# One load of output weights, a grouped early projection and useless matmuls at the end of a decode kernel

## The chip, the cores and the metric

The kernel runs on one core of a Trainium2 chip. The metric is the device time of one execution in microseconds (us). Beside it every run lists the *span* of the core, from its first to its last instruction. The device time is about 2.0 us longer than the span, and that difference scatters by some tenths from run to run, so where a few tenths matter this text compares spans.

PE is the engine that multiplies matrices, DVE and ACT are the two that copy and do elementwise work, SP issues the loads. "Granted clock" is the share of full speed that PE's clock was given; in the records it is only ever 1.0 or 0.5. I call PE *warm* at 1.0 and *cold* at 0.5.

## The reference

A decode step of attention with a key and value cache, then a small MLP, both behind adaptive layer norms.

```python
# B=8, D=512, 32 query heads, 8 key/value heads, 8192 positions, head size 128, F=1792
h = layernorm(x) * (1 + ca) + sa
q = (h @ wq)                               # 32 heads of 128
p = softmax(q @ k_cache^T * Dh**-0.5)      # k_cache, v_cache: 8 x 8 x 8192 x 128 bf16
x = x + ga * ((p @ v_cache) @ wo)          # wo: 4096 x 512 = 4 MB
h = layernorm(x) * (1 + cb) + sb
x = x + gb * (relu(h @ w1 + b1)**2 @ w2 + b2)
```

The two caches are 268 MB, and everything else is 15 MB.

## The kernel before

Each batch has four key units and four value units of 4 MB each, loaded through a ring of four slots. I count units from 0, so the last batch ends with value units 2 and 3. Value unit 3 of the last batch comes in four smaller loads (chunks of 64, 32, 16 and 16 tiles), and the MLP weights (`ring<-in_B_w`) are loaded behind it. The output projection for the first three units is done early, while the last unit is still arriving.

```python
# the output weights: 24 heads in 4 KB runs, 8 heads in 1 KB runs
d_woe = dma("sync", s_woe, lambda e: e.dma_start(
    wo_e, A_wo[0:24 * DH, :].rearrange("(g p j) n -> p g (j n)", g=6, p=128)))
d_wo = dma("sync", s_wo, lambda e: e.dma_start(
    wo_sb[:, 24:32, :], A_wo[24 * DH:, :].rearrange("(h dh) n -> dh h n", dh=DH)))
# ...
def pe_stream(n, at):            # n useless 512-column matmuls, to keep PE busy
    # ...
def project(k_oP):               # early projection: 96 matmuls of 32 columns
    for g in range(6):
        for j in range(4):
            for k in range(KT):
                op("tensor", lambda e, g=g, j=j, k=k: e.matmul(
                    attn_w[:, k, :, :], wo_sb[:, 4 * g + j, k * 128:(k + 1) * 128], wide(oP[:, j, g, :]),
                    start=(g == 0 and j == 0 and k == 0), stop=False, skip_group_check=True),
                    [k_oP, d_woe])
# ... a value unit (all but the very last): 32 matmuls of 512 columns in four column groups
for m in range(32):
    cg = m % 4
    t = op("tensor", lambda e, p=p, m=m, cg=cg, vt=vt, Obank=Obank: e.matmul(
        Obank[32 * cg:32 * (cg + 1), :], lhs[:, p, 32 * m:32 * m + 32],
        vt[:, 4 * m:4 * m + 4, :], start=(m < 4), stop=(m >= 28), tile_position=(0, 32 * cg)), ...)
# ... behind it a copy to SBUF, four selection matmuls, and (last batch, unit 2) the early projection
    if lastb and p == NP - 2:
        project(early([norm_last, k_all] + stg_free + hold))
# ... the last value unit: 24 wide matmuls (chunks 0 and 1), 16 narrow (chunk 2), 16 narrow (chunk 3)
    direct(96, 112, 2, True, False)
    # ...
    t = direct(112, 128, 3, False, True)
    for x in range(8):           # final projection: the last 8 heads
        for k in range(KT):
            k_attn = op("tensor", ...)
# ... layer norm, W1 (56 matmuls), squared ReLU, W2 (56 matmuls, wait for the last loads), output
```

## Time and profile before

| | before |
|---|---|
| device time, first three runs | 670.03 us (669.75 to 670.32) |
| span of the profiled run | 668.1 us |
| bytes moved, mean rate | 283.86 MB, 425 GB/s |
| PE busy | 74% of the span |

From the page of the kernel before: the busy share of the DMA engines in 40 slices of the span (a digit is tenths, 9 is 90% or more), and the packet counts.

```profile
DMA  9999999999999999999999999999999999999996
...
DMA packets 12961, 283.86 MB, mean 425 GB/s; under 512 B 1266, under 2 KB 2323, under 8 KB 4372
```

The DMA engines are busy from the first slice to the last but one. So a microsecond saved inside the loop on PE is worth nothing, and one saved in the stream of bytes is worth a microsecond, provided that the work behind the last byte keeps up.

The output-weight loads of the kernel before, from the view of DMA issues (size, median us from issue to landing):

```profile
wo_sb<-in_A_wo_dram SPq DMA_DIRECT2D x1, 3072.0 KB, 45.5
wo_sb<-in_A_wo_dram SPq DMA_DIRECT2D x1, 1024.0 KB, 48.0
```

The end of the span decides. PE's timeline there, kernel before (start us, duration us, engine, line, operation, output<-inputs, shapes, count, and in brackets the idle time before the group and what ended it):

```profile
644.90 1.91 PE L607 MATMUL PS<-ring,Pm 128*32 128x512 bf16 x32 [1.49 <-DMA ring<-in_A_v_cache_dram]
...
649.09 2.69 PE L517 MATMUL PS<-KTb,wo_sb 128*128 128x32 bf16 x96 [0.51 <-DVE KTb L511]
...
651.90 1.74 PE L659 MATMUL PS<-ring,Pm 128*32 128x512 bf16 x16
...
656.47 0.99 PE L682 MATMUL PS<-oTn,wo_sb 128*128 128x8 bf16 x32 [0.29 <-DVE oTn L677]
...
664.07 1.01 PE L730 MATMUL PS<-KTb,ring 128*128 128x8 bf16 x24 [0.67 <-DMA ring<-in_B_w_dram]
```

Value unit 2 (L607) starts when its load lands at 644.86; the early projection (L517) follows, then the last value unit (L659), the final projection (L682), and W2 (L730), which waits 0.67 us for its weights. The chain that ended last in the kernel before says the same (start us, length us, what):

```profile
648.00 16.02 DMA ring<-in_B_w_dram
664.02 0.05 issue
664.07 0.59 PE PS L730 x16
```

So the loads end the span, and PE is close behind them. The granted clock around this place, kernel before, from the table of windows with the windows cut where the clock may change (window and length in us; busy us and instruction counts of PE, PEld, DVE, ACT, POOL; granted clock; DMA share; GB/s):

```profile
646.52:649.93 3.41, 1.71 (x61) 1.22 (x54) 1.25 (x3) 0.00 (x0) 0.00 (x0) 1.00 0.96 402
649.93:653.34 3.41, 3.41 (x90) 2.37 (x85) 0.00 (x0) 0.00 (x0) 0.00 (x0) 0.50 1.01 403
653.34:656.75 3.41, 2.83 (x77) 1.95 (x70) 0.88 (x2) 0.00 (x0) 0.00 (x0) 1.00 1.02 405
```

A window in which PE was half busy (1.71 of 3.41 us) is followed by one at clock 0.50, and a fully busy one by 1.00.

### The profile page before, as it was taken

The numbers are of one execution on the slowest core, as the hardware profiler recorded it, in microseconds if no ns is written. First come the engines' busy times: TensorE is split into PE (matmuls) and PEld (weight loads), VectorE is DVE, ScalarE is ACT, GpSimd is POOL, SyncE is SP. The second block draws the span as 40 slices with busy tenths as digits, with TensorE's granted clock in tenths as the row PEclk, the third lists the DMA queues.
The fourth block names the chain that finished last, engine by engine and source line by source line (L and its number), as shares of the span: only waits on it lengthen the run. The fifth ranks groups of instructions, "written<-read, shape, count | busy, mean of one in ns | idle before, by whom it ended". The sixth has DMA issues, their size and how long they took to land.

```text
span 668.1 us, 15500 instructions
## 1 busy us (share of the span) xinstructions
PE 494.0 (74%) x7076; PEld 339.1 (51%) x7076; DVE 301.6 (45%) x569; ACT 258.7 (39%) x289; POOL 17.7 (3%) x71
## 2 busy tenths in 40 slices
PE   3494964898639983699638985499746996389866
PEld 2383731685228741577317752287414773177534
DVE  1262741466216651367315672167513673156622
ACT  2151640466205660166404661066502664046610
POOL 7300000000000000000000000000000000000000
PEclk9696996799869997599968998699977999579996
DMA  9999999999999999999999999999999999999996
GB/s 376 435 403 438 420 429 438 428 430 430 439 428 432 428 439 428 432 430 438 428 434 428 438 428 434 428 438 428 434 428 438 430 432 428 438 434 430 426 420 263
DMA packets 12961, 283.86 MB, mean 425 GB/s; under 512 B 1266, under 2 KB 2323, under 8 KB 4372
## 3 DMA queue, kind: packets, MB, share of 16 engines
q1 hardware_dynamic: 12900, 283.65, 99.1%
q8 instruction: 10, 0.16, 0.1%
q10 hardware_dynamic: 48, 0.02, 0.0%
q14 instruction: 3, 0.02, 0.0%
HBM read 283.66 MB, written 0.01 MB: 425 GB/s over the span
## 4 chain that ended last, share of the span: by engine, by line
PE 51%; DMA 37%; ACT 7%; DVE 4%; SPq 1%; issue 1%
PE PS L467 36%; DMA ring<-in_A_k_cache_dram 34%; PE PS L484 9%; ACT P_sb L553 5%; DMA ring<-in_B_w_dram 2%; PE PS L607 2%; ACT KTb L472 1%; SPq L642 1%; DVE m L491 1%; DVE O_sb L613 1%; PE PS L565 1%; PE PS L457 1%; DVE Pm L579 0%; PE PS L585 0%; DVE rhs_r L582 0%
## 5 line engine op out<-in xcount | busy, mean ns | idle before, releaser
L472 ACT ACTIVATE KTb<-PS 128x1024 bf16<-128x1024 bf16 x192 | 196.5, 1024 | 332.9 <-PE PS L467 332.9
L467 PE MATMUL PS<-IDENT,ring 128*128 128x128 bf16 x4096 | 268.1, 228 | 50.5 <-DMA ring<-in_A_k_cache_dram 50.5
L467 PEld LDWEIGHTS PS<-IDENT,ring 128*128 128x128 bf16 x4096 | 247.4, 102 | 99.2 <-DMA ring<-in_A_k_cache_dram 51.7
L474 DVE COPY KTb<-PS 128x1024 bf16<-128x1024 bf16 x320 | 210.0, 688 | 144.7 <-PE PS L467 142.7
L607 PE MATMUL PS<-ring,Pm 128*32 128x512 bf16 x992 | 78.3, 472 | 55.5 <-DMA ring<-in_A_v_cache_dram 54.7
L484 PE MATMUL PS<-KTb,Qb 128*32 128x512 bf16 x1024 | 79.1, 386 | 4.5 <-ACT KTb L472 4.5
L613 DVE CAST O_sb<-PS 128x512 bf16<-128x512 f32 x31 | 21.4, 692 | 127.4 <-PE PS L607 127.4
L607 PEld LDWEIGHTS PS<-ring,Pm 128*32 128x32 bf16 x992 | 28.5, 112 | 91.0 <-DMA ring<-in_A_v_cache_dram 56.0
L553 ACT ACTIVATE P_sb<-PS,negm 128x1024 bf16<-128x1024 f32 x32 | 35.2, 1112 | 20.2 <-DVE negm L549 20.2
L565 PE MATMUL PS<-IDENT,P_sb 128*128 128x128 bf16 x256 | 19.9, 221 | 16.0 <-ACT P_sb L553 16.0
L579 DVE COPY Pm<-PS 64x512 bf16<-64x512 bf16 x48 | 20.2, 421 | 25.0 <-PE PS L565 24.5
L457 PE MATMUL PS<-IDENT 128*128 128x512 bf16 x120 | 31.2, 380 | 0.0
L617 PEld LDWEIGHTS PS<-SEL,O_sb 128*128 128x128 bf16 x124 | 5.2, 98 | 44.6 <-DVE O_sb L613 44.6
L565 PEld LDWEIGHTS PS<-IDENT,P_sb 128*128 128x128 bf16 x256 | 14.4, 98 | 24.1 <-ACT P_sb L553 24.1
L617 PE MATMUL PS<-SEL,O_sb 128*128 128x8 bf16 x124 | 8.0, 170 | 24.8 <-DVE O_sb L613 24.8
L484 PEld LDWEIGHTS PS<-KTb,Qb 128*32 128x32 bf16 x1024 | 15.5, 94 | 21.1 <-ACT KTb L472 8.5
L491 DVE TENSOR_REDUCE m<-PS 128x1 f32<-128x512 f32 x32 | 22.1, 689 | 6.6 <-PE PS L484 6.6
L457 PEld LDWEIGHTS PS<-IDENT 128*128 128x128 bf16 x120 | 10.3, 103 | 10.0 <-issue 3.4
L624 DVE TENSOR_TENSOR oTn<-PS,rinv 128x8 f32 x31 | 6.0, 194 | 14.2 <-PE PS L617 14.2
L472 ACT ACT_TABLE_LOAD x8 | 10.3, 1283 | 3.2 <-issue 3.2
L561 ACT ACTIVATE Pm<-PS 64x512 bf16<-64x512 bf16 x16 | 9.5, 592 | 2.7 <-PE PS L565 2.6
L393 PE MATMUL PS<-ring,KTb 128*32 128x512 bf16 x56 | 7.2, 627 | 3.5 <-DMA ring<-in_A_wq_dram 3.3
(125 smaller groups left out, 100.8 us busy)
## 6 DMA issues: line engine op xcount, KB each, us to landing
ring<-in_A_k_cache_dram SPq DMA_DIRECT2D x32, 4096.0 KB, 33.0
ring<-in_A_v_cache_dram SPq DMA_DIRECT2D x31, 4096.0 KB, 27.7
ring<-in_A_wq_dram SPq DMA_DIRECT2D x1, 4096.0 KB, 19.8
ring<-in_w_mod_dram SPq DMA_DIRECT2D x1, 3072.0 KB, 10.5
wo_sb<-in_A_wo_dram SPq DMA_DIRECT2D x1, 3072.0 KB, 45.5
ring<-in_A_v_cache_dram SPq DMA_DIRECT2D x1, 2048.0 KB, 22.4
ring<-in_B_w_dram SPq DMA_DIRECT2D x3, 512.0 KB, 18.5
ring<-in_B_w_dram SPq DMA_DIRECT2D x1, 1344.0 KB, 17.7
```

What stands on the lines that cost most here:

```text
L457: ts = [op("tensor", lambda e: e.matmul(bank(at).rearrange("p (a r) -> p a r", a=4), IDENT[:, :], rhs)) for _ in range(n)]
L467: t = op("tensor", lambda e, j=j, i=i: e.matmul(STG[j][:, i, :], src[:, 32 * k + 8 * j + i, :], IDENT[:, :], is_transpose=True), [loaded[n ...
L472: stg_free[j] = op("scalar", lambda e, j=j, dst=dst: e.activation(dst, STG[j], ACT.Copy), [t])
L474: stg_free[j] = op("vector", lambda e, j=j, dst=dst: e.tensor_copy(dst, STG[j]), [t])
L484: t = op("tensor", lambda e, hf=hf, q=q, rhs=rhs: e.matmul(PS[32 * q:32 * (q + 1), k, :], Qb[:, 2 * p + hf, :], rhs, start=(p == 0 and hf ...
L491: return op("vector", lambda e: e.tensor_reduce(m4[:, k:k + 1], bank(k), AX.X, ALU.max), [t])
L553: exps.append(op("scalar", lambda e, k=k: e.activation(P_sb[:, k, :, :, :], bank(k).rearrange("p (i x) -> p i x", i=8).unsqueeze(2).to_bro ...
L565: t = op("tensor", lambda e, k=k, i=i: e.matmul(STG[k][:, i, :], P_sb[:, k, i, :, :].rearrange("p h x -> p (h x)"), IDENT[:, :], is_transp ...
L579: done.append(op("vector", lambda e, dst=dst, frm=frm: e.tensor_copy(dst, frm), [t, k_pm]))
L607: t = op("tensor", lambda e, p=p, m=m, cg=cg, vt=vt, Obank=Obank: e.matmul(Obank[32 * cg:32 * (cg + 1), :], lhs[:, p, 32 * m:32 * m + 32], ...
L613: t = op("vector", lambda e, osb=osb, Obank=Obank: e.tensor_copy(osb, Obank), [t])
L617: t = op("tensor", lambda e, i=i, osb=osb, oT_ps=oT_ps: e.matmul(oT_ps, osb[:, i * 128:(i + 1) * 128], SEL[:, i, :], start=(i == 0), stop= ...
```

## The change

The intent, in four parts:

1. All 4 MB of output weights come in one load of 4 KB runs. The 1 KB runs go.
2. Five useless matmuls behind value unit 1 in every batch keep PE busy before value unit 2.
3. The early projection becomes 24 matmuls of 512 columns in four column groups, a copy, and four fp32 matmuls with a selection matrix.
4. The third chunk of the last value unit goes through four more wide matmuls instead of 16 narrow ones. The last eight heads now need the permutation too, because their weights lie permuted.

```diff
-        d_woe = dma("sync", s_woe, lambda e: e.dma_start(
-            wo_e, A_wo[0:24 * DH, :].rearrange("(g p j) n -> p g (j n)", g=6, p=128)))
         d_wo = dma("sync", s_wo, lambda e: e.dma_start(
-            wo_sb[:, 24:32, :], A_wo[24 * DH:, :].rearrange("(h dh) n -> dh h n", dh=DH)))
+            wo_sb[:, :, :].rearrange("p (g j) n -> p g (j n)", j=4),
+            A_wo.rearrange("(g p j) n -> p g (j n)", g=8, p=128)))
 # ... cut ...
         def project(k_oP):
             for g in range(6):
                 for j in range(4):
-                    for k in range(KT):
-                        op("tensor", lambda e, g=g, j=j, k=k: e.matmul(
-                            attn_w[:, k, :, :], wo_sb[:, 4 * g + j, k * 128:(k + 1) * 128], wide(oP[:, j, g, :]),
-                            start=(g == 0 and j == 0 and k == 0), stop=False, skip_group_check=True),
-                            [k_oP, d_woe])
+                    t = op("tensor", lambda e, g=g, j=j: e.matmul(
+                        bank(7)[32 * j:32 * (j + 1), :], oP[:, g, :, :].rearrange("p j b -> p (j b)"),
+                        wo_sb[:, 4 * g + j, :], start=(g == 0), stop=(g == 5), tile_position=(0, 32 * j)),
+                        [k_oP, d_wo])
+            return op("vector", lambda e: e.tensor_copy(proj, bank(7)), [t])
 # ... cut ...
+                    if p == NP - 3:
+                        pe_stream(5, 4)
 # ... cut: the last value unit ...
-                    for m in range(24):
+                    for m in range(28):
 # ...
+                            for k in range(KT):
+                                op("tensor", lambda e, k=k: e.matmul(
+                                    attn_ps[:, k, :], proj[:, 128 * k:128 * (k + 1)], SELP[:, :],
+                                    start=(k == 0), stop=False, skip_group_check=True), [k_proj])
-                    direct(96, 112, 2, True, False)
 # ...
+                    k_oP = permute(3, 4, oP[:, 6:8], [t])
 # ... cut: the final projection reads oP in place of oTn; the bias rows share one tile
```

## The prediction

> What bounds the kernel now. The DMA stream. On the page the DMA row is 9 tenths in every slice but the last, 425 GB/s over 668.1 us; the table of windows gives a DMA share of 0.97 to 1.02 in nearly every 12 us. PE is busy 74% and in each batch waits for a key or value load (chain of waits: "DMA ring<-in_A_k_cache_dram" 34% of the span, about 24 us each batch). So changes inside the batch loop are off the critical path. What counts is how long the 16 DMA engines have bytes to move, and the few us after the last weight lands. In the timeline of the end, the last matmuls twice wait for B_w (0.18 and 0.67 us), the last weights land near 664.6, PE ends at 665.7. The end is still DMA-bound, PE under 1 us behind.
>
> What the change does.
> 1. One output-weight load. Today 3 MB go in 4 KB runs and 1 MB in 1 KB runs (1024 packets). In the packet records a 1 KB packet takes 48 ns, a 4 KB one 159. 1024 x 48 / 16 = 3.07 us against 256 x 159 / 16 = 2.54: 0.5 us less, or 0.4 to 0.5 allowing for overlap. The stream has no slack, so this passes to the end. The Trainium skill, "DMA: Bandwidth & Descriptors", section "Why small descriptors are slow", gives a fixed cost per packet; this trace agrees (4 x 48 = 192 against 159).
> 2. Five useless matmuls behind value unit 1, about 1.25 us in a 1.5 us idle gap of PE. In the loop: free. At the end they may keep the granted clock at 1.0 where it now falls to 0.5 (649.9 to 653.3); they can delay unit 2 by 0.3 us.
> 3. Early projection: 96 matmuls (2.69 us) become 24 of 512 columns in four column groups (estimate from L607, 32 in 1.91 us: 1.4 us), plus a 0.7 us copy and four fp32 matmuls (L416, four such: 1.0 us). PE saves little net.
> 4. Third chunk: 16 direct matmuls (0.57 us) become 4 wide ones (0.3). But the last heads now need the permutation too: 16 matmuls 0.32 us, copy 0.3 us and handoffs, behind the last value chunk. I put the start of the final projection at 656.3 to 656.8 (now 656.47): no gain and little loss, inside the slack to the B_w loads.
> 5. About 60 fewer matmuls after the loop. PE's instruction fetches (16 KB, about 1.07 us of one DMA engine each) at 653.1, 659.2, 663.7 shift. The landings show the engines spread over 3.1 us at the end, one late through such a fetch. If the second fetch avoids a late engine, up to 1 us more is won.
>
> On the critical path: about 0.45 us of item 1, perhaps part of 5. Predicted 669.5 us against 670.03; range 668.6 to 670.2. Chances: faster by over 2% 0.005, within 2% 0.99, slower 0.005.
>
> What would show it. 1 KB packets gone, one wo_sb load of 4096 KB; value landings 0.4 to 0.5 us earlier from about 60 us on; DMA share unchanged; last B_w landing near 664.2; early projection 24 wide matmuls, about 1.4 us; granted clock higher around 650.
>
> What would make it wrong. The chain behind the last value chunk is longer than I think (fp32 matmuls, permutation), so PE, not B_w, ends the span: the gain vanishes or turns to +0.5. A fetch falls otherwise on the slowest engine: 1 us either way. PE was the true limit at the end and gets shorter: up to 1.5 us gain.

## The result, and the profile after

| | before | after |
|---|---|---|
| device time, median of four runs | 670.08 us (669.75 to 670.32) | 670.05 us (669.63 to 672.52) |
| spans of the changed kernel's four runs | | 670.3, 667.9, 668.1, 667.8 us |
| ratio after/before, 95% interval | | 1.0008 [0.9983, 1.0032] |

A ratio is the mean time of one kernel's fast runs over the mean of the other's in the same rounds, so it is not quite the ratio of the medians. The time did not move: the forecast gain of about 0.5 us is missing. What is new is scatter. The kernel before has spans of 667.8 to 668.9 us in all 46 fast runs; the changed one goes from below that to well above it, and the profile was taken of the slowest run, 670.3 us. That is part of the finding, not noise to be left out.

The change did what it should to the stream. From the page after, and the view of DMA issues:

```profile
DMA packets 12176, 283.85 MB, mean 423 GB/s; under 512 B 1250, under 2 KB 1283, under 8 KB 3588
...
wo_sb<-in_A_wo_dram SPq DMA_DIRECT2D x1, 4096.0 KB, 47.6
```

The 1 KB packets are gone (2323 packets under 2 KB before, 1283 now). From the packet records I summed the times of the 1 KB packets of the output weights and of all 4 KB packets (640 of these belong to the MLP weights, in both kernels) and divided by the 16 engines: 3.25 (1 KB) + 14.33 (4 KB) = 17.58 us before, 16.98 us after, 0.6 us less. The last of the 16 engines lands value unit 2 at 644.86 us before and at 644.08 us after, 0.8 us earlier in these two profiles (644.24 and 644.44 in two later ones of the changed kernel).

PE's timeline at the end, kernel after:

```profile
641.76 1.24 PE L463 MATMUL PS<-IDENT 128*128 128x512 bf16 x5
644.12 3.58 PE L608 MATMUL PS<-ring,Pm 128*32 128x512 bf16 x32 [1.12 <-DMA ring<-in_A_v_cache_dram]
...
649.97 1.76 PE L517 MATMUL PS<-wo_sb,KTb 128*32 128x512 bf16 x24 [0.51 <-DVE KTb L512]
...
651.86 1.90 PE L662 MATMUL PS<-ring,Pm 128*32 128x512 bf16 x16
...
654.23 1.88 PE L673 MATMUL PS<-SELP,KTb 128*128 128x8 f32 x8
656.03 1.47 PE L662 MATMUL PS<-ring,Pm 128*32 128x512 bf16 x12
...
660.00 1.01 PE L690 MATMUL PS<-KTb,wo_sb 128*128 128x8 bf16 x32 [0.37 <-DVE KTb L512]
...
665.68 1.65 PE L737 MATMUL PS<-KTb,ring 128*128 128x8 bf16 x56 [0.97 <-DVE KTb L733]
```

Value unit 2 starts 0.8 us earlier than before, yet the final projection (L690) starts at 660.00 instead of 656.47, and W2 (L737) no longer waits for weights at all. The same 32 matmuls of value unit 2 that took 1.91 us take 3.58. The chain that ended last, kernel after, is PE's work and its handoffs from the landing of value unit 2 on:

```profile
616.09 27.99 DMA ring<-in_A_v_cache_dram
644.12 3.60 PE PS L608 x32
...
654.30 1.81 PE PS L673 x8
...
665.68 1.67 PE PS L737 x56
```

And the windows, cut at the clock steps of this run:

```profile
640.79:644.20 3.41, 1.49 (x17) 0.58 (x17) 0.88 (x2) 0.00 (x0) 0.00 (x0) 1.00 0.91 389
644.20:647.61 3.41, 3.41 (x32) 1.03 (x32) 0.00 (x0) 0.00 (x0) 0.00 (x0) 0.50 0.99 423
647.61:651.02 3.41, 1.72 (x44) 0.92 (x44) 1.24 (x3) 0.00 (x0) 0.00 (x0) 1.00 0.97 400
651.02:654.43 3.41, 3.41 (x43) 1.36 (x36) 0.69 (x1) 0.00 (x0) 0.00 (x0) 0.50 1.03 407
```

Value unit 2, and then nearly all of the last unit and the fp32 selection, fell into cold windows. The five useless matmuls left the window ahead of value unit 2 at 1.49 us busy of 3.41.

My theory from here on: the stream did gain its half microsecond, and the new chain of PE work is more sensitive to a cold clock than the old one, so that in some runs PE ends the span later than the loads and gives the gain back. The rivals: the useless matmuls delay value unit 2; the new chain is too long even when warm (permutation, copy, fp32); the single load is not worth anything.

### The profile page after: what moved, and what is told of

The parts are those of the page before. It is cut to its first block, busy times and chain, and to the rows that moved or that the text cites. A ratio compares the mean times of both kernels' runs of the same rounds, so it can differ in the third digit from the quotient of the medians.

```text
span 670.3 us, 15469 instructions
## 1 busy us (share of the span) xinstructions
PE 498.0 (74%) x7056; PEld 340.4 (51%) x7056; DVE 302.5 (45%) x571; ACT 258.7 (39%) x289; POOL 18.4 (3%) x76
## 2 busy tenths in 40 slices
DMA packets 12176, 283.85 MB, mean 423 GB/s; under 512 B 1250, under 2 KB 1283, under 8 KB 3588
## 4 chain that ended last, share of the span: by engine, by line
PE 51%; DMA 38%; ACT 6%; DVE 4%; issue 1%; SPq 0%; DVEq 0%
PE PS L473 35%; DMA ring<-in_A_k_cache_dram 32%; PE PS L490 9%; ACT P_sb L554 5%; DMA ring<-in_A_v_cache_dram 4%; PE PS L608 3%; DMA ring<-in_A_wq_dram 2%; ACT KTb L478 1%; DVE O_sb L614 1%; DVE m L497 1%; PE PS L566 1%; PE PS L662 0%; PE PS L463 0%; DVE Pm L580 0%; PE PS L586 0%
## 5 line engine op out<-in xcount | busy, mean ns | idle before, releaser
L608 PE MATMUL PS<-ring,Pm 128*32 128x512 bf16 x992 | 72.2, 442 | 55.2 <-DMA ring<-in_A_v_cache_dram 54.2
L463 PE MATMUL PS<-IDENT 128*128 128x512 bf16 x160 | 41.1, 379 | 0.0
L566 PEld LDWEIGHTS PS<-IDENT,P_sb 128*128 128x128 bf16 x256 | 14.4, 98 | 24.1 <-ACT P_sb L554 24.1
L463 PEld LDWEIGHTS PS<-IDENT 128*128 128x128 bf16 x160 | 13.5, 101 | 12.9 <-issue 3.4
L478 ACT ACT_TABLE_LOAD x8 | 10.3, 1283 | 3.2 <-issue 3.2
## 6 DMA issues: line engine op xcount, KB each, us to landing
ring<-in_B_w_dram SPq DMA_DIRECT2D x3, 512.0 KB, 19.9
```

Of the source, the lines that this page charges most:

```text
L463: ts = [op("tensor", lambda e: e.matmul(bank(at).rearrange("p (a r) -> p a r", a=4), IDENT[:, :], rhs)) for _ in range(n)]
L478: stg_free[j] = op("scalar", lambda e, j=j, dst=dst: e.activation(dst, STG[j], ACT.Copy), [t])
L566: t = op("tensor", lambda e, k=k, i=i: e.matmul(STG[k][:, i, :], P_sb[:, k, i, :, :].rearrange("p h x -> p (h x)"), IDENT[:, :], is_transp ...
```

## The experiments

18 experiments ran, in five sessions, on 15 different kernels (a_same2, a_nostream2 and a_bf16proj2 repeat one). Within a session all share a chip and the runs of the kernel before; from session to session the chip changes. A time is the median of the device times. A "mean span" is over all the fast runs; one run of the kernel before, 709.73 us at a mean clock of 0.656, is left out.

| kernel | runs | time us | mean span (range) | before, same session | ratio [95%] |
|---|---|---|---|---|---|
| a_same | 5 | 670.75 | 668.62 (667.6–669.1) | 668.20 | 1.0003 [0.9989, 1.0017] |
| b_oneload | 5 | 669.55 | 667.52 (667.3–667.7) | 668.20 | 0.9992 [0.9979, 1.0006] |
| a_bf16proj | 5 | 669.32 | 667.50 (667.4–667.7) | 668.20 | 0.9989 [0.9976, 1.0003] |
| a_nostream | 5 | 669.40 | 667.74 (667.4–668.6) | 668.20 | 0.9995 [0.9981, 1.0008] |
| b_w2cut | 5 | 669.67 | 668.00 (667.2–668.9) | 668.19 | 0.9994 [0.998, 1.0007] |
| a_w2cut | 5 | 669.59 | 667.32 (666.1–668.3) | 668.19 | 0.9985 [0.9971, 0.9998] |
| b_group | 5 | 670.29 | 668.62 (668.1–669.8) | 668.19 | 1.001 [0.9996, 1.0023] |
| b_wide | 5 | 670.51 | 668.24 (667.8–668.8) | 668.19 | 1.0003 [0.999, 1.0017] |
| a_stream9 | 5 | 670.00 | 668.10 (667.6–668.7) | 668.16 | 0.9996 [0.9981, 1.001] |
| a_bf16_stream9 | 5 | 669.76 | 667.72 (667.4–668.1) | 668.16 | 0.9993 [0.9979, 1.0007] |
| a_oldproj | 5 | 669.92 | 667.90 (667.6–668.3) | 668.16 | 0.9996 [0.9982, 1.001] |
| b_oneload_perm | 5 | 669.77 | 668.08 (667.6–668.9) | 668.16 | 0.9996 [0.9982, 1.001] |
| a_same2 | 6 | 669.78 | 668.37 (667.5–670.5) | 668.26 | 1.0003 [0.9988, 1.0018] |
| a_nostream2 | 6 | 671.29 | 669.17 (667.4–670.9) | 668.26 | 1.0012 [0.9997, 1.0028] |
| a_bf16proj2 | 5 | 669.71 | 667.86 (667.6–668.5) | 668.26 | 0.9994 [0.9981, 1.0007] |
| a_bf16_nostream | 5 | 669.20 | 667.44 (666.9–668.5) | 668.26 | 0.9984 [0.9971, 0.9997] |
| a_fill | 5 | 669.75 | 667.60 (667.5–667.7) | 668.41 | 0.9989 [0.9975, 1.0002] |
| a_bf16_fill | 5 | 669.41 | 667.72 (667.4–668.3) | 668.41 | 0.9991 [0.9978, 1.0005] |

All results were within tolerance except those of a_w2cut and b_w2cut, which are wrong. Only two intervals exclude 1, so single ratios settle little here; the argument rests on the traces and on which spans occur. There is one profile for each kernel, and in several cases that profile is of a warm run and the other runs' clocks are known only as a mean.

A second table, of the profiles. All times but the first two columns count from the landing of value unit 2, so that the stream's gain is taken out:

| profile | unit 2 lands us | its 32 matmuls us | final projection starts | W2 starts | last load lands | span us |
|---|---|---|---|---|---|---|
| before | 644.86 | 1.91 | +11.62 | +17.27 | +19.80 | 668.1 |
| b_w2cut | 645.10 | 3.58 | +13.36 | +19.01 | (+16.90, cut) | 668.8 |
| after | 644.08 | 3.58 | +15.92 | +21.60 | +18.85 | 670.3 |
| a_same | 644.24 | 3.47 | +14.49 | +20.18 | +18.86 | 669.1 |
| a_same2 | 644.44 | 1.91 | +11.65 | +17.32 | +19.70 | 667.6 |
| a_nostream | 644.17 | 3.25 | +12.90 | +18.53 | +18.86 | 667.4 |
| a_stream9 | 644.40 | 1.91 | +13.76 | +19.44 | +18.83 | 668.5 |
| a_oldproj | 644.15 | 1.91 | +13.29 | +18.98 | +19.91 | 667.8 |
| a_bf16_nostream | 644.16 | 3.61 | +14.09 | +19.70 | +18.85 | 668.5 |
| a_fill | 644.25 | 1.91 | +11.85 | +17.48 | +19.88 | 667.6 |

### The changed kernel again: a_same and a_same2

```diff
 (no edit)
```

> The changed kernel again, unaltered, with more rounds. Theory T (the DMA stream ends about 0.5 us earlier, but the PE chain behind value unit 2 has become longer and now ends the span): median 669.7 to 670.3, with a scatter over 1 us because the PE chain feels the phase of the granted clock; last weight landing 1 us or more before PE needs it. Rival R (the DMA stream did not get shorter, the profiled run was an outlier): scatter as before, about 0.5 us, and PE waits for the last weights as before.

> The changed kernel a third time, as the partner of the next three on one chip. Theory P (the end is a race of the DMA end and a PE chain that half-clock windows lengthen by up to 3 us, by chance of phase): spans from 667.5 to 670, mean near 668.5. If the slow runs so far were an accident of two sessions: spans 667.5 to 668.0.

The spans were 669.1, 669.0, 668.9, 667.6, 668.5 and 667.6, 670.5, 667.5, 668.0, 667.8, 668.8 us. With the first four, that is 15 runs with a mean of 668.49, a standard deviation of 0.94 and 8 runs at or below 668.1; the 46 runs of the kernel before have 668.25 and 0.31. So the same kernel both gains and loses against the kernel before.

The two profiles happened to catch two kinds. That of a_same was cold at value unit 2, like the first one. That of a_same2 was warm up to 654.32 us. PE's timeline there, kernel a_same2:

```profile
644.48 1.91 PE L608 MATMUL PS<-ring,Pm 128*32 128x512 bf16 x32 [1.34 <-DMA ring<-in_A_v_cache_dram]
...
648.66 1.48 PE L517 MATMUL PS<-wo_sb,KTb 128*32 128x512 bf16 x24 [0.51 <-DVE KTb L512]
...
651.77 1.06 PE L673 MATMUL PS<-SELP,KTb 128*128 128x8 f32 x8
...
656.09 1.01 PE L690 MATMUL PS<-KTb,wo_sb 128*128 128x8 bf16 x32 [0.37 <-DVE KTb L512]
...
663.55 1.00 PE L737 MATMUL PS<-KTb,ring 128*128 128x8 bf16 x24 [0.77 <-DMA ring<-in_B_w_dram]
```

The final projection starts at 656.09 and W2 waits for weights again. Group by group, the slow profile (after) minus this one: value unit 2 3.58 − 1.91 = 1.67; grouped projection 1.76 − 1.48 = 0.28; 16 wide matmuls 1.90 − 1.05 = 0.85; selection 1.88 − 1.06 = 0.82; 12 wide matmuls 1.47 − 0.83 = 0.64. The sum is 4.26 us, and the final projection started 15.92 − 11.65 = 4.27 us later. No wait, no copy and no handoff is left to blame. Of the 4.26 us only 1.10 lie in groups that the change brought in (projection and selection); the rest lies in wide matmuls, most of which the kernel before has too. For a_same against a_same2 the groups give 1.56 + 0.46 + 0.85 = 2.87, and the start is 2.84 us later. This is correlation in three profiles; a_fill below is the intervention.

One thing hides in this comparison. The start at +11.65 looks like that of the kernel before, +11.62, but the profile before was not at full clock here: its 16 wide matmuls of the last unit took 1.74 us, against 1.05 in a_same2. Without these 0.69 us the old chain would start its final projection near +10.9 (an estimate). At equal clock the new chain is thus about 0.7 us longer. One reason stands in the waits for the copy in front of the four selection matmuls of the last unit, a_same2 first, then before, where 16 narrow matmuls fill part of the wait:

```profile
654.39 0.27 PE L679 MATMUL PS<-SEL,O_sb 128*128 128x8 bf16 x4 [0.80 <-DVE O_sb L677]
...
655.52 0.26 PE L673 MATMUL PS<-SEL,O_sb 128*128 128x8 bf16 x4 [0.30 <-DVE O_sb L670]
```

The other is the permutation, 0.7 us by b_oneload and b_oneload_perm below. The shorter third chunk and projection give part of this back. As long as PE is warm the 0.7 us stay inside the slack, but they are missing from it when PE is cold.

The two windows ahead of and at value unit 2, kernel a_same2:

```profile
640.67:644.08 3.41, 1.66 (x17) 0.50 (x9) 0.89 (x2) 0.00 (x0) 0.00 (x0) 1.00 0.92 394
644.08:647.49 3.41, 2.17 (x36) 0.93 (x36) 0.69 (x1) 0.00 (x0) 0.00 (x0) 1.00 0.96 408
```

1.66 of 3.41 us busy kept the clock, and in the slow profile 1.49 lost it. The five useless matmuls put the kernel near this edge.

### The single load without the rest: b_oneload and b_oneload_perm

```diff
 # b_oneload: the kernel before, both waits on the one load; the weights of the last
 # eight heads then lie permuted and nothing undoes it, so the result is wrong by design
+        d_woe = d_wo = dma("sync", s_wo, lambda e: e.dma_start(
+            wo_sb[:, :, :].rearrange("p (g j) n -> p g (j n)", j=4),
+            A_wo.rearrange("(g p j) n -> p g (j n)", g=8, p=128)))
 # b_oneload_perm: the same with the permutation of the last heads; no useless matmuls,
 # the old projection, the third chunk narrow
```

> Before with the one output-weight load alone (wrong result on purpose: the last eight heads meet permuted rows; instruction counts unchanged). Theory T: 0.4 to 0.6 us faster than before (669.5 to 669.7), PE still waits for the last weights at the end, last landing near 664.1. Rival R: within 0.2 us of before.

> Before with the one load done rightly (last heads permuted too), old projection, old third chunk, no useless matmuls. The permutation adds about 0.7 us behind the last value chunk. Theory C: DMA end 0.5 us earlier, but with unit 2 at half clock in most runs (no stream) the chain is about 0.7 us longer than in before: median 669.6 to 670.3, scatter about 1 us, that is, the gain of the wrong-result one-load kernel is partly lost. Rival: 669.5 like that kernel, because the permutation hides behind the last weights.

b_oneload has a mean span of 667.52 against 668.20, 0.7 us less, with all five runs (667.3 to 667.7) below the lowest run of the kernel before (667.8). Value unit 2 landed at 644.39. (Its result is wrong, but it differs so little that it passed the tolerance.) The load alone thus gives what the prediction's sum said, and the rival that it is worth nothing falls.

b_oneload_perm is the load with what it needs to be right. Its mean span is 668.08 (one run at 668.9) against 668.16, so most of the gain was not seen. In its profile the final projection started at +12.75, 0.85 us later than in b_oneload (+11.90). Value unit 2 itself took 0.23 us longer (2.63 against 2.40, both partly cold). The permutation's matmuls, copy and handoffs can be read directly, at full clock in both profiles: from the end of the last chunk's matmuls to the start of the final projection it is 0.29 us in b_oneload (656.00 to 656.29) and 0.97 us here (656.14 to 657.11), 0.7 us more on a chain that has little slack.

### Without the useless matmuls: a_nostream and a_nostream2

```diff
-                    if p == NP - 3:
-                        pe_stream(5, 4)
```

> The changed kernel without the five useless matmuls. Theory T with the stream helping the clock: 0.5 us or more slower than the changed kernel or with more scatter. If the stream does nothing or delays unit 2: same or up to 0.3 us faster. In the loop nothing should change either way.

> The changed kernel without useless matmuls again. If the stream costs at the end, as 5 against 9 runs suggest: mean span 0.4 to 1.0 us under that of the changed kernel (667.6 to 668.0). If that was chance of phase: the same mean within 0.3 us.

The first time this looked like a gain over the changed kernel (667.74 against 668.62 in the same session), the second time like a loss (669.17 against 668.37). Pooled, 11 runs average 668.52 and the changed kernel's 15 runs 668.49. The second forecast, a gain of 0.4 to 1.0 us without them, failed. So no effect of the useless matmuls shows at the end (the difference of these two means has a standard error of some 0.4 us, an estimate from the scatter of the runs), and I had to drop the rival that they delay value unit 2. The profile of a_nostream shows that a cold value unit 2 alone need not cost anything: it took 3.25 us, all behind it was warm, and the span was 667.4. In the loop they do what they were put there for: value unit 2 was warm in 7 of 7 loop batches of the first profile after, in 1 of 7 of that before. In the last batch, five were too few: over the seven profiles that have them, value unit 2 was cold three times.

### Shorter weights: b_w2cut and a_w2cut

```diff
-                            for i, (a, z, j) in enumerate(((0, 4, 4), (4, 8, 4), (8, 12, 4), (12, 14, 2)))]
+                            for i, (a, z, j) in enumerate(((0, 4, 4), (4, 8, 4)))]
+                    d_w2 = d_w2 + [d_w2[1], d_w2[1]]
```

The last 6 of W2's 14 tiles are not loaded. The result is wrong (relative error 0.077). This makes the loads end 2 to 3 us earlier and leaves PE's work as it is, so whatever time remains is PE's.

> Before, with the last two loads of the second dense weight (768 KB, about 1.9 us of the stream) left out, so that those rows are stale (wrong on purpose). It shows how far PE trails the last weights. If before is bound by the DMA end, as the prediction said: the three waits in its last matmuls go (0.18, 0.67 and about 0.4 us), so 1.0 to 1.4 us faster, span near 667.0, and PE ends the span. If PE bounds it already: within 0.3 us.

> The same cut in the changed kernel. Theory T (there the PE chain behind value unit 2 ends the span): median within 0.3 us of the changed kernel (span 667.3 to 670), scatter kept, because nothing waits for the cut loads. If DMA still bounds it: 1 us or more faster, as in before.

Neither gave one number. a_w2cut had 666.1 and 666.5 in two runs and 667.8, 667.9 and 668.3 in three; b_w2cut 667.2 and 667.3 in two, 667.8, 668.8 and 668.9 in three. I had expected a_w2cut within 0.3 us of the changed kernel, and that is a miss: its two fastest runs are 1.0 us or more below every run of the changed kernel (667.5 at least), so in its good runs the changed kernel *is* bound by the loads. Its chain would end near 666.4 by an estimate from a_same2 (the profiles of after and a_same end 10.3 to 10.4 us behind the start of their final projection, and that of a_same2 starts at 656.09), and the fast runs are there. b_w2cut gained the expected microsecond in two of its runs; that these were the warm ones is likely, but only one run was profiled. That profile is of a cold one:

```profile
645.14 3.58 PE L607 MATMUL PS<-ring,Pm 128*32 128x512 bf16 x32 [2.26 <-DMA ring<-in_A_v_cache_dram]
...
651.01 2.68 PE L517 MATMUL PS<-KTb,wo_sb 128*128 128x32 bf16 x96 [0.51 <-DVE KTb L511]
```

Value unit 2 is cold as in the changed kernel, and the final projection starts only 1.74 us later than in the profile before (13.36 − 11.62), of which 1.67 is value unit 2. The 96 narrow matmuls take 2.68 us, against 2.69 in the profile before. That alone does not compare cold with warm, because the mean granted clock under them was 0.68 here and 0.66 there. The profile of b_oneload does: its 96 lay wholly in a cold stretch. Kernel b_oneload, PE's timeline and the window of the group:

```profile
649.19 2.74 PE L515 MATMUL PS<-KTb,wo_sb 128*128 128x32 bf16 x96 [0.51 <-DVE KTb L509]
...
649.19:651.93 2.74, 2.74 (x98) 2.70 (x99) 0.00 (x0) 0.00 (x0) 0.00 (x0) 0.50 1.00 405
```

In a_oldproj (below) the same group took 2.61 us at a mean clock of 0.91. No profile has it wholly warm.

### The parts alone: b_group, b_wide and a_oldproj

```diff
 # b_group: the kernel before (two loads, no useless matmuls, third chunk narrow)
 # with the grouped projection alone (made from the changed kernel by undoing the rest;
 # the bias rows stay in one shared tile)
+                    t = op("tensor", lambda e, g=g, j=j: e.matmul(
+                        bank(7)[32 * j:32 * (j + 1), :], oP[:, g, :, :]..., wo_sb[:, 4 * g + j, :], ...
+                                    attn_ps[:, k, :], proj[:, 128 * k:128 * (k + 1)], SELP[:, :], ...
 # b_wide: the kernel before with the third chunk in wide matmuls alone
-                    for m in range(24):
+                    for m in range(28):
-                    direct(96, 112, 2, True, False)
 # a_oldproj: the changed kernel with the early projection as before (96 narrow matmuls, no selection)
```

> Before with the grouped early projection alone (24 wide matmuls, fp32 copy, four fp32 matmuls), loads, third chunk and the last heads as before, no useless matmuls. Theory T: the replacement is no shorter (1.5 to 1.9 plus 1.0 to 1.9 us against 2.7) and doubles where the clock is at half, so runs lie between before and 1.5 us over it, scatter over 0.7 us. If the grouped projection is cheap at either clock: within 0.2 us of before, scatter as before.

> Before with the third chunk in wide matmuls alone. 16 direct matmuls go, four wide ones come; the chain behind the last chunk gets at most 0.3 us shorter and DMA ends the span: within 0.2 us of before under every theory. A rise of over 0.3 us would show that waiting for the third chunk before the copy costs.

> The changed kernel with the old early projection (96 narrow matmuls accumulating in place), all else as changed. If the grouped projection with its four fp32 matmuls is what lengthened the chain: 0.4 to 1.0 us faster than the changed kernel, 669.2 to 669.8, since the narrow matmuls take about 27 ns each at either clock. If the permutation of the last heads or the wide third chunk is to blame: as slow as the changed kernel.

b_wide changes nothing (668.24 against 668.19). b_group is 0.4 us longer (668.62 against 668.19, one run at 669.8), without any change in the bytes. Its profile had value unit 2 warm, and still the final projection started at +13.08 instead of +11.62, because the clock fell behind unit 2. Kernel b_group:

```profile
649.00 1.70 PE L519 MATMUL PS<-wo_sb,KTb 128*32 128x512 bf16 x24 [0.51 <-DVE KTb L514]
...
650.82 1.90 PE L662 MATMUL PS<-ring,Pm 128*32 128x512 bf16 x16
...
653.18 1.88 PE L673 MATMUL PS<-SELP,KTb 128*128 128x8 f32 x8
```

So the clock is not lost at value unit 2 only: here it falls in the stretch of short handoffs behind it, and the grouped projection with its fp32 selection lies just there. a_oldproj, which puts the old projection into the changed kernel, comes to 667.90 against 668.16, better than the changed kernel's mean of 668.49. That fits, but weakly: its median of 669.92 is just outside the forecast 669.2 to 669.8, its interval holds 1, and in its profile the 16 and 12 wide matmuls of the last unit were cold too (1.90 and 1.47 us), so that the final projection started at +13.29.

### A longer stream, and a copy in bf16: a_stream9, a_bf16proj, a_bf16proj2, a_bf16_stream9, a_bf16_nostream

```diff
 # a_stream9
-                        pe_stream(5, 4)
+                        pe_stream(9, 4)
 # a_bf16proj, a_bf16proj2: copy of the projection and selection matrix in bf16
-        SELP = sb("SELP", [128, B], FP32)
+        SELP = sb("SELP", [128, B], BF16)
-        proj = KF[:, 4096:5120].bitcast(FP32)
+        proj = KF[:, 4096:4608]
 # a_bf16_stream9, a_bf16_nostream: both edits; the bf16 copy without useless matmuls
```

> The changed kernel with nine useless matmuls in place of five. In the traces so far the clock fell to half after a 3.41 us window in which PE was busy under about half, and stayed full above about 0.5; five useless matmuls leave the worst window before value unit 2 at 0.44 to 0.46. Theory C (the changed kernel loses to half-clock windows in the chain from value unit 2 on): unit 2 takes 1.9 us in all eight batches, median 0.3 to 1.0 us below the changed kernel (669.3 to 669.8). Rival L (the chain is simply longer in work, the clock does not decide): within 0.2 us of the changed kernel although unit 2 is warm.

> The changed kernel with the copied projection and its selector in bf16 instead of fp32: the four fp32 matmuls (8 instructions, 1.88 us in the cold profile, estimated 1.0 us warm) become 4 of about 0.12 us in all. Theory T: 0.6 to 1.7 us faster than the changed kernel, near 669.0, until the last weights bound it again. Rival R (DMA bounds the end): within 0.2 us of the changed kernel. Result stays correct.

> The bf16 projection copy again, to see whether its tight spans hold. Theory P: with 0.75 to 1.6 us taken from the chain, DMA ends the span in nearly every run: spans 667.3 to 667.8, at least 0.5 us under the changed kernel in the mean. If the first five were luck: up to 669.

> The changed kernel with both mends: bf16 projection copy and nine useless matmuls. Both theories: the DMA end bounds it, span 667.4 to 667.6 in every run, 669.2 to 669.4, no gain over the bf16 kernel alone; PE waits for the last weights. Candidate for the best version.

> bf16 projection copy and no useless matmuls. Theory P: as the bf16 kernel, 667.3 to 667.8; a best version without the stream. If the stream is what keeps the bf16 kernel tight: scatter up to 668.5.

Nine useless matmuls made value unit 2 warm in 8 of 8 batches of the profile, and did not help: 668.10 against 668.16, and the median of 670.00 misses the forecast of at most 669.8. PE's timeline, kernel a_stream9, shows why:

```profile
645.11 1.91 PE L608 MATMUL PS<-ring,Pm 128*32 128x512 bf16 x32
...
651.50 1.90 PE L662 MATMUL PS<-ring,Pm 128*32 128x512 bf16 x16
```

The load had landed at 644.40 and the matmuls waited behind the nine until 645.11, 0.7 us. And the clock was only lost a window later, so that the 16 wide matmuls of the last unit took 1.90 us, and the final projection started at +13.76. My theory in its first form, "value unit 2 is cold", was too narrow: the stretch of handoffs behind value unit 2 loses the clock as well.

The bf16 copy did well: 667.50 and 667.86, ten runs with a mean of 667.68, the highest 668.5. (The first five lay within 0.3 us, the second five did not: five tight runs are a small sample.) With nine useless matmuls as well, a_bf16_stream9 gave 667.72, and two of its five runs (667.9 and 668.1) lie above the forecast of 667.4 to 667.6 in every run. Without useless matmuls it reached the shortest span of any right kernel, 666.9 us in three of five runs (the others 668.0 and 668.5, so both ends miss the forecast of 667.3 to 667.8), and the only interval of a right kernel clear of 1 (0.9984 [0.9971, 0.9997]). The selection is recorded as four matmuls and takes 0.26 us (forecast 0.12) in place of 1.06 (warm) or 1.88 (cold). In the warm profile of a_bf16proj that wins nothing, because PE then waits 0.57 us for the third chunk and the final projection starts at +11.53 (a_same2: +11.65); in a cold run it would take up to 1.6 us (1.88 − 0.26, an estimate: no profile has it cold) out of a chain that is too late. How much of the gain is this and how much is luck with the clock I cannot tell: the profiles of a_bf16proj and a_bf16proj2 had value unit 2 warm, and that of a_bf16_nostream (span 668.5) had it cold, with the final projection at +14.09. The bf16 copy shortens the chain; it does not keep the clock.

### PE kept busy through the whole end: a_fill and a_bf16_fill

```diff
-                        pe_stream(5, 4)
+                        pe_stream(7, 4)
+                    if p == NP - 2:
+                        pe_stream(2, 4)        # behind the selection of unit 2
+                    if p == NP - 2:
+                        pe_stream(3, 4)        # behind the 32 matmuls of unit 2
         def project(k_oP):
+            pe_stream(2, 4)                    # behind the permutation
```

All useful work is that of the changed kernel; there is only more useless work, 14 matmuls in place of 5 in the last batch (12 in the others). If the length of the chain or the useless matmuls were at fault, this must be slower. If the cold clock is at fault, the slow runs must vanish.

> The changed kernel, its useful work untouched, with more useless matmuls in the holes of the end: seven before value unit 2, three while its result is copied, two behind its selection, two behind the permutation. They should keep every 3.41 us window over half busy until the projection is done. Theory P (the lost time is half clock on the wide and fp32 matmuls, not their work at full clock): unit 2 in 1.9 us, the grouped projection in 1.5 and the fp32 selection in 1.0 us, all spans within 667.4 to 668.1, mean 0.5 us or more under the changed kernel's 668.5. Rival L (the chain is too long even at full clock): spans over 668.2 in a third of the runs or more, with the clock at full in the profile.

> The same filling with the bf16 projection copy. Both theories: DMA ends every run; spans 667.0 to 667.8, mean within 0.2 us of the bf16 kernel without filling (667.7), because nothing on PE is then limiting.

The five spans of a_fill are 667.6, 667.5, 667.7, 667.6 and 667.6 us. The mean is 0.9 us below that of the changed kernel, and the scatter is gone. Against the kernel before in the same session it is 668.41 − 667.60 = 0.8 us shorter, and against all 46 runs 0.65. Windows at the same place as above, kernel a_fill:

```profile
646.51:649.93 3.42, 3.37 (x51) 1.19 (x50) 1.24 (x3) 0.00 (x0) 0.00 (x0) 1.00 0.96 401
649.93:653.34 3.41, 3.41 (x62) 2.20 (x54) 0.69 (x1) 0.00 (x0) 0.00 (x0) 1.00 1.03 406
```

The window that was cold in the kernel before, behind 1.71 us of work, is warm here, behind 3.37. PE's timeline, kernel a_fill:

```profile
648.75 1.48 PE L518 MATMUL PS<-wo_sb,KTb 128*32 128x512 bf16 x24
...
651.85 1.06 PE L678 MATMUL PS<-SELP,KTb 128*128 128x8 f32 x8
...
656.10 0.97 PE L695 MATMUL PS<-KTb,wo_sb 128*128 128x8 bf16 x32 [0.38 <-DVE KTb L512]
...
663.54 1.02 PE L742 MATMUL PS<-KTb,ring 128*128 128x8 bf16 x24 [0.78 <-DMA ring<-in_B_w_dram]
```

The final projection is at 656.10, and W2 waits 0.78 us for its weights: the span is bound by the stream again, with the stream's gain in it. The new chain with all its work is in place, and at full clock it does not end the span. Without the cold clock the loss is gone: that is the cause shown by an intervention. The cold clock acted on wide and fp32 matmuls, not on the new ones alone (see the split of the 4.26 us above). Two limits: the changed kernel was not run on the same chip beside a_fill, and the clock at the end is known for one of the five runs.

a_bf16_fill is no better (667.72). That fits the theory that once the loads end the span, a shorter PE chain wins nothing. But its spans are 667.4, 668.3, 667.6, 667.9 and 667.4 us, two of them above the forecast 667.0 to 667.8. Its profile is of a 667.4 run, so what made the 668.3 is open, and filling is not shown to remove every slow run.

### What the loads do at the end

The last column but one of the table of profiles has two values, +18.8 to +18.9 and +19.6 to +19.9. They go with PE's instruction fetches, 16 KB packets that occupy one DMA engine for about 1.07 us. In the changed kernel and its variants with the grouped projection, where the second fetch behind the loop came at +16.9 to +17.5 (a_same2, a_bf16proj, a_fill and others) the last weights landed at +19.6 or later; where it came at +17.7 or later (after, a_same, a_stream9, b_group and others) they landed at +18.8 to +18.9, 0.7 to 1.1 us earlier. With the old projection the fetches lie elsewhere (+14.4 in the profile before) and the last landing is at +19.5 to +19.9. So it looks as if a chain that is early pulls its fetch into the last loads and pays part of its own gain. This is read from the order of events in the 18 profiles with all loads, and it is not shown: a fetch at +17.7 also starts before the last landing, and no experiment moved a fetch alone.

## Why the prediction was right or wrong

**The gain of the stream: right.** Item 1 said 0.5 us. The packet records show 0.6, b_oneload 0.7, and a_fill, which lets the gain through, 0.65 to 0.8. The last weights were forecast near 664.2 us; they landed at 662.93 in the first profile after and at 664.14 in a_same2.

**The failed step** is in items 3 and 4: "PE saves little net", and "I put the start of the final projection at 656.3 to 656.8 (now 656.47): no gain and little loss, inside the slack to the B_w loads". At full clock the start is right: 656.09 in a_same2. What failed is "inside the slack". The durations of the new work were taken from warm matmuls (1.91 us at L607 and 1.0 us at L416, both at clock 1.0), and the 656.47 that they were compared with came from a partly cold stretch. At the changed kernel's cold ends the final projection started at 658.7 (a_same) and 660.0 us (after). The runs put this in its place:

| group | warm us | cold us |
|---|---|---|
| value unit 2, 32 wide | 1.91 | 3.58 |
| early projection before, 96 narrow | 2.61 (a_oldproj, mean clock 0.91) | 2.74 (b_oneload, clock 0.50) |
| early projection after, 24 wide | 1.48 | 1.76–1.94 (partly cold), 2.75 (cold, a_nostream2) |
| first chunk of the last unit: 16 wide | 1.05 | 1.90 |
| selection, fp32, recorded as 8 | 1.06 | 1.88 |
| second and third chunk: 12 wide | 0.83 | 1.47 |

The change swaps work whose time hardly depends on the clock for work whose time nearly doubles when it is cold, in the stretch behind value unit 2, and the wide matmuls around it, old and new, are hit as well. The Trainium skill, "TensorE: Matmul & The Clock Gate", section "Wait — 56ns, not 53.3ns?", says that the start-to-start time of small matmuls has a floor of about 25 ns. The trace agrees: 2.61 us / 96 = 27 ns in a_oldproj at a mean clock of 0.91, and 2.74 / 96 = 29 in b_oneload at 0.50.

How much of it reaches the time follows from the slack. In a_same2 the chain would have ended near 666.4 us against a span of 667.6, 1.2 us of slack. The cold excess of 2.8 us in a_same and 4.3 us in after overruns it by 1.6 and 3.1 us. (With the earlier landing of value unit 2 taken off, this equals the extra span of these runs. That is no second proof, since the 666.4 was worked out from the tails of the same two profiles; the two fast runs of a_w2cut, 666.1 and 666.5, are an independent one.) The old chain at full clock would have ended near 666.1, by the same kind of estimate (644.86 + 10.9 + 10.3), 2.0 us ahead of its span. So the change had used up some 0.8 us of slack before any cold clock. In the kernel before the cold excess was 0.7 us in its own profile and 2.4 in b_w2cut (1.67 in value unit 2 and 0.76 in the next 16 wide matmuls), which just overruns 2.0 us: this fits spans that stay within 668.9. Averaged, the changed kernel loses 0.9 us (668.49 against a_fill's 667.60), all that the stream gains and a little more.

**Item 2** said that the useless matmuls "may keep the granted clock at 1.0" at the end. They did so in the loop, where it is worth nothing, and not reliably at the end, where it counts: over the seven profiles with five of them, PE was 1.49 to 1.58 us busy in the deciding window when the clock was then lost (after, a_same, a_w2cut) and 1.66 to 2.37 us when it was kept. The feared delay of value unit 2 (0.3 us) did not occur with five; with nine it was 0.7.

**Item 5** said that up to 1 us hangs on the fetches. The last landings do differ by up to 1.1 us together with them, but the other way round than hoped: of the changed kernel's own profiles the fast one (a_same2) has the early fetch and the late landing, and the slow ones (after, a_same) the reverse, so it damps the gain. That the fetch is the cause is not shown.

**What would make it wrong** named the right outcome, that "PE, not B_w, ends the span", with half of the cause: the chain is 0.7 us longer in itself, but that alone did not end the span (a_same2, a_fill). The cold clock did. The profile before already showed a cold window in this place, and with it the missing question: which instructions take nearly twice as long there?

What stays open: why value unit 2 of the last batch was cold in 3 of 7 profiles with five useless matmuls when it was warm in nearly all loop batches of the same kernels. The phase of the clock windows against the kernel would explain a mixture, but no run set that phase. And with differences of 0.1%, that a_bf16_nostream or a_fill beats both kernels is likely, not certain: the intervals are [0.9971, 0.9997] and [0.9975, 1.0002].

## What to carry to other kernels

At the end of a stream-bound kernel two clocks run, that of the last loads and that of the work behind the last large load: cost each new instruction there at the lower granted clock too, because here wide and fp32 matmuls nearly doubled and very narrow ones hardly moved. Compare starts and slack at equal clock, or a cold stretch in the reference hides a longer chain. Useless matmuls help only where they carry PE over *every* window up to the last useful work, so fill the handoffs as well and check the windows cut at the clock's own steps: a window over half busy was no guarantee at the end (see below). When a change moves the median little but widens the scatter, look for two kinds of run and profile both before you explain the mean.

## What the Trainium skill lacked or had wrong

- "TensorE: Matmul & The Clock Gate", Part 1 (The HAM clock gate): it has two clock states and windows of 3413 ns, and this case agrees (only 1.0 and 0.5, in steps of 3.41 us). Its table in "Why this matters for your kernels" asks for no PE-idle gap over about 3 us. That is not enough: here the clock fell behind a window with PE 1.49 of 3.41 us busy, whose longest gap was about 1.1 us. Over 20 profiles, counting the warm windows from 60 to 660 us, 255 of 264 with PE under half busy were followed by a drop, and only 24 of 2457 over half; no rise followed one below 0.77. But behind 645 us, at the end that counts here, 23 of 42 windows over half busy lost the clock too (2.83 of 3.41 us in before), so the busy share of the profile is not the whole rule there; what else counts is open.
- The same page, "Wait — 56ns, not 53.3ns?", has the floor for small matmuls but not its consequence: 96 narrow matmuls took 2.61 to 2.74 us at either clock, while 32 wide ones took 1.91 or 3.58.
- I found no page that gives the time of a small fp32 matmul at either clock: four of 8 columns, recorded as eight, took 1.06 us warm and 1.88 cold.
- "Runtime: NRT & Kernel Launch", section "Instruction fetch mechanics", has the 16 KiB blocks and calls crossing one mostly hidden. The size agrees. Here a fetch took one DMA engine for about 1.07 us, and with a saturated stream an earlier one went with a last landing 0.7 to 1.1 us later (+19.6 to +19.9 against +18.8 to +18.9).
- "DMA: Bandwidth & Descriptors", section "Why small descriptors are slow (HBM only)", has a fixed cost per packet; it gives none for 1 KB against 4 KB runs. Here a 1 KB packet took 48 ns and a 4 KB one 159, 33 ns in four of 192 saved by joining them.
